# Two score passes of the next batch ahead of a w_in stage in a fused attention and GELU-MLP kernel

## The chip, the cores and the metric

The kernel runs on one core of one Trainium2 chip. The metric is the device time of one execution in microseconds (us). Beside it stands one profiled execution: its trace has the start and duration of every instruction on TensorE (PE; its weight loads are PEld), VectorE (DVE), ScalarE (ACT), GpSimd (POOL) and the DMA issues of SyncE (SP).

## What is computed

The inputs are q, k and v of 8 batches x 12 heads x 448 tokens x 64, and two weight matrices. Attention with normalised q and k is followed by two matrix products with an exact GELU between them.

```python
q_n = q / (np.linalg.norm(q, axis=-1, keepdims=True) + 1e-06)
k_n = k / (np.linalg.norm(k, axis=-1, keepdims=True) + 1e-06)
scores = np.matmul(q_n, k_n.transpose(0, 1, 3, 2)) / tau
attn = softmax(scores)                      # over the last axis
x = (attn @ v).transpose(0, 2, 1, 3).reshape(B * S, H * D)   # 3584 x 768
h = x @ w_in                                # 768 x 2048
g = 0.5 * h * (1 + erf(h / sqrt(2)))
out = g @ w_out                             # 2048 x 768, float32
```

## The kernel before

**Units of work.** Batches are counted from 0 to 7 and quads (four heads) from g = 0 to 23, three a batch. A quad's q and k are prepared in a chain: load (L129, SP), squares (L156, POOL), sums of squares (L165, DVE), logarithm and the exponential of half of it (L172 and L181, ACT), adding 1e-6 and the reciprocal (L190 POOL, L192 DVE), scaling to bf16 (L208, two POOL instructions) and a DMA transpose (L220, SP). Quad g is unit g+1 in the code, since quad 0 is cut in two. Units that share the small instructions L172 to L192 are a "group".

A quad's scores are 7 passes, 21 in a batch. A pass (L246) is 4 matmuls of 64x64 that run side by side into one pair of PSUM banks, and one exponential on ACT (L253), which frees the pair. There are 8 banks: pairs 0, 1 and 2 and two single banks ("mm"). After a quad's 7 exponentials `both` makes the row sums (L275, 16 matmuls of 128x32, into an mm bank), the values (L289, 28 matmuls of 64x64, into a pair) and on DVE the reciprocals and the two products with x (L297 to L323).

**Stages.** `attention(b)` alternates score passes of batch b with runs of matmuls of the second product (L352, "op", called fill), left over from batch b-1. A run takes as many as `plan` says: 96 in all for odd b, 128 for even b. Then `first(b)` is the w_in stage: 96 matmuls (L642, "hp") in 16 column blocks and 16 GELUs (L678). The first few blocks (`ahead`) do their first four steps of six before any does the last two, which need the batch's last quad. PE runs all of this in the order in which the code issues it. Exponential and GELU need different ACT tables, so that ACT loads a table ahead of the w_in stage (L634) and behind it (L687).

**Order around the change.** Every engine runs its instructions in program order and waits only on semaphores; tiles come from pools of a few buffers (q and k 4, scaled quads 3, transposed quads 3, exponentials 15). `upto(f, n)` issues step f up to item n at that point. Before, `group(b, k)` issues passes in eight parts of 3, 3, 3, 2, 3, 3, 2, 2; part 0 stands behind the w_in stage of b-1 and the others lie among the six runs of `attention(b)`. Batch 0 has an order of its own (L405), and during it POOL issues the casting loads of the weights wi (L381) and wo (L388) and of v (L141), while SP issues the loads of q and k.

Of the kernel before, what the change touches and what calls it, by code (L numbers as in the profile page):

```python
# [16 lines left out]
def kernel(  # L17
# [20 lines left out]
    NQ = H // 4  # L38
# [66 lines left out]
    def pair(i, name):  # L105
        pool = third[0] if i == 2 else ps_st
        return pool.tile([128, 2, 512], F32, tag=f"st{i}", name=name)
# [3 lines left out]

    units = [(0, 0, 1), (0, 1, 2)] + [(g, 0, 2) for g in range(1, NG)]
    NU = len(units)
    groups = [[n] for n in range(NQ + 2)] + [[NQ + 2, NQ + 3]]
    for n in range(2 * NQ + 1, NU, NQ):
        groups += [[n, n + 1], [n + 2]]
    shapes = [[len(gr), 2, units[gr[0]][2] - units[gr[0]][1], C] for gr in groups]
    place = {u: (n, j) for n, gr in enumerate(groups) for j, u in enumerate(gr)}
    qk_t, v_t, sq_t, nq_t, rn_t, qkb_t, qkT_t, pt_t = {}, {}, {}, {}, {}, {}, {}, {}
# [139 lines left out]
    def sums(g, chunks=range(C)):  # L259
        for c in chunks:  # L260
            if c == 0:
                bank_t[g, "sm"] = ps_acc.tile([128, 512], F32, tag="sm", name=f"sm{g}") if g < NQ else \
                    mm_tile(f"sm{g}", aside=0)
            for s in range(2):
                if g < NQ:
                    nc.tensor.matmul(bank_t[g, "sm"][64 * s:64 * (s + 1), :S],
                                     lhsT=ones2.rearrange("p a h r -> p (a h r)"), rhs=pt_t[g, s, c],
                                     start=(c == 0), stop=(c == C - 1), tile_position=(0, 64 * s))
                    continue

                half = 2
                for i in range(2) if c == half else ((c - (c > half)) % 2,):
                    r = 32 * (2 * s + i)
                    cols = slice(i * S // 2, (i + 1) * S // 2) if c == half else slice(0, S)
                    nc.tensor.matmul(bank_t[g, "sm"][r:r + 32, cols], lhsT=ones, rhs=pt_t[g, s, c][:, cols],  # L275
                                     start=(c < 2), stop=(c >= C - 2), tile_position=(0, r))
# [18 lines left out]
    def turned(g):  # L295
        tr = rcp.tile([128, NB, 32], F32, tag="tr", name=f"tr{g}")
        nc.vector.transpose(tr.rearrange("p b r -> p (b r)"), bank_t.pop((g, "sm"))[:, :S])  # L297
        bank_t[g, "tr"] = tr.rearrange("p b (k r) -> p k b r", k=2)

    def inverted(g):  # L300
        tr = bank_t.pop((g, "tr"))
        if g < NQ:
            su = tr[:, :, :, 0]
        else:


            for j in range(4):
                o = j ^ 1
                nc.vector.tensor_reduce(tr[32 * j:32 * (j + 1), :, :, 1], tr[32 * o:32 * (o + 1), :, :, 0:1],  # L309
                                        mybir.AxisListType.X, ALU.add)  # L310
            su = rcp.tile([128, 2, NB], F32, tag="su", name=f"su{g}")
            nc.vector.tensor_reduce(su, tr[:, :, :, 0:2], mybir.AxisListType.X, ALU.add)
        rc = bank_t[g, "rc"] = rcp.tile([128, 2, NB], F32, tag="rc", name=f"rc{g}")
        nc.vector.reciprocal(rc, su)

    def spread(g, h):
        rs = rcp.tile([128, NB, 32], F32, tag=f"rs{h}", name=f"rs{g}_{h}")
        nc.vector.transpose(rs, bank_t[g, "rc"][:, h].to_broadcast([128, NB, 32]))  # L318
        rs_t[g, h] = rs.rearrange("p b r -> p (b r)")
# [5 lines left out]
    def both(g, p):  # L325
        sums(g)
        turned(g)
        inverted(g)
        spread(g, 0)
        spread(g, 1)  # L330
        values(g, p=p)
        normalise(g, 0)
        normalise(g, 1)
# [60 lines left out]
    def upto(f, n, last=None):  # L394
        last = {load_qk: NG, load_v: NV, root: len(groups), load_wi: 4, load_wo: 4}.get(f, NU)
        while done.get(f, 0) < min(n, last):
            done[f] = done.get(f, 0) + 1
            f(done[f] - 1)
# [173 lines left out]
        done.update({square: 6, reduce: 5, root: 5, scale: 5, transposes: 5})  # L572


    passes = [(n, c) for n in range(NQ) for c in range(C)]
    group_pairs = [(0, 1, 2), (0, 1, 2), (0, 1, 2), (1, 2), (1, 2, 0), (1, 2, 0), (2, 0), (2, 0)]

    def group(b, k):
        n0 = sum(len(p) for p in group_pairs[:k])
        for p, (n, c) in zip(group_pairs[k], passes[n0:]):  # L580
            scores(b * NQ + n, ((0, c), (1, c)), p)
            exps(b * NQ + n, ((0, c), (1, c)))

    def attention(b, fill):
        fill = list(fill)
        plan = {96: (20, 13, 13, 12, 16, 22), 128: (24, 18, 20, 18, 22, 26)}[len(fill)]
        parts = iter(plan)

        def run():
            for _ in range(next(parts)):  # L590
                fill.pop(0)()

        x_t[b] = xp.tile([128, KD, S], BF16, tag="x", name=f"x{b}")
        g0, nu = b * NQ, (b + 1) * NQ + 1
        run()
        for n in (nu - 1, nu):
            upto(scale, n)
            upto(transposes, n)
        group(b, 1)
        upto(square, nu + 1)  # L600
        run()
        group(b, 2)
        both(g0, 0)
        upto(load_v, b + 3)
        if b == 1:
            upto(load_qk, g0 + NQ + 2)
        group(b, 3)
        upto(square, nu + 2)
        run()
        group(b, 4)  # L610
        upto(reduce, nu + 1)
        upto(load_qk, g0 + NQ + 3)
        run()
        group(b, 5)
        both(g0 + 1, 1)
        group(b, 6)
        run()
        group(b, 7)
        upto(reduce, nu + 2)
        n = 2 * b + 4  # L620
        if n < len(groups):
            logs(n)
            roots(n)
        run()
        both(g0 + 2, 1)
        if n < len(groups):
            inverses(n)
            done[root] = n + 1

    def first(b):  # L630
        sb, hf = divmod(b, 2)
        if hf == 0:
            g_t[sb] = gp.tile([128, KF, 2 * S], BF16, tag="g", name=f"g{sb}")
        nc.scalar.preload_act_table_set(GELU_SET)  # L634
        nu = (b + 1) * NQ + 1
        hps = {}
        pairs = (0, 2) if b else (0, 2, 6, 8)
        ahead = 4 if b else 5

        def mm(m, kds):  # L640
            for kd in kds:
                nc.tensor.matmul(hps[m], lhsT=wi[:, kd, m * 128:(m + 1) * 128],  # L642
                                 rhs=x_t[b][:, kd, :], start=(kd == 0), stop=(kd == KD - 1))

        def bank(m):
            if m in pairs:
                p = (2, 0)[m // 2] if b else (1, 0, 1, 0)[pairs.index(m)]
                st = pair(p, f"hp{b}_{m}")
                hps[m], hps[m + 1] = st[:, 0, :S], st[:, 1, :S]
            elif m not in hps:  # L650
                hps[m] = mm_tile(f"hp{b}_{m}")[:, :S]

        for m in range(ahead):
            bank(m)
            mm(m, range(KD - 2))
        if b == 0:
            upto(square, nu + 3)
        for n in (nu + 1, nu + 2) if b else (nu + 1,):
            upto(scale, n)
            upto(transposes, n)  # L660
        if b:
            upto(load_qk, (b + 1) * NQ + 5)
        else:
            upto(load_wo, 4)
        upto(square, nu + 3)
        upto(reduce, nu + 3)
        for m in range(ahead):
            mm(m, range(KD - 2, KD))
        for m in range(KF):
            if b == 0 and m == 8:  # L670
                for i in range(2):
                    transposes(4, i)
                    copies(4, i)
            if m >= ahead and (m == 0 or m - 1 not in pairs):
                for k in range(m, m + 1 + (m in pairs)):
                    bank(k)
                    mm(k, range(KD))
            nc.scalar.activation(g_t[sb][:, m, hf * S:(hf + 1) * S], hps.pop(m), AF.Gelu)  # L678
            if b == 0 and m == 5:
                nc.scalar.preload_act_table_set(EXP_SET)  # L680
                upto(root, 6)
                nc.scalar.preload_act_table_set(GELU_SET)
                upto(scale, nu + 2)
                upto(transposes, nu + 2)
                upto(load_qk, 2 * NQ + 1)
        if b + 1 < B:
            nc.scalar.preload_act_table_set(EXP_SET)  # L687
            group(b + 1, 0)
            upto(root, 2 * b + 6)

    upto(load_qk, 1)
    nc.scalar.preload_act_table_set(EXP_SET)
# [7 lines left out]
    fill = []  # L700
    for b in range(B):
# [12 lines left out]
        fill = [f for t, ni in todo if t not in tail for f in second_pieces(sb, t, ni)]  # L714
# [38 lines left out]
```

## Time and profile before

| what | value |
|---|---|
| time, median of 4 runs | 418.26 us (417.54 to 418.69) |
| the profiled execution: its time | 418.69 us |
| its span, first to last instruction | 416.9 us |
| granted TensorE clock | 0.998 |
| busy: PE, ACT, DVE, POOL | 98%, 59%, 45%, 40% |
| start of the w_in stage of batch 0 to 3 | 32.71, 80.68, 132.05, 178.44 us |
| start of the w_in stage of batch 4 to 7 | 229.81, 276.20, 327.57, 373.96 us |

From one w_in start to the next it takes 51.37 us where the fill is 128 and 46.39 us where it is 96, each time alike from the second on; the first such stretch, from batch 0 to batch 1, is 47.97 us.

A line of the timeline gives start, duration, engine, line and operation, output<-inputs, shapes and count; in brackets is the idle time ahead of it and what ended it. Ends of matmuls are modelled, so that stretches on PE are taken from one start to the next. In the list of DMA queues, q0 holds what POOL issues and q1 what SP issues.

### The profile page before, as it was taken

How to read it: one execution, taken by the hardware profiler on the slowest of the kernel's cores; microseconds unless marked ns; L12 is line 12 of the kernel's file. 1: busy time of each engine (PE TensorE's matmuls, PEld its weight loads, DVE VectorE, ACT ScalarE, POOL GpSimd, SP SyncE). 2: the span in 40 equal slices, each digit the busy share in tenths (PEclk: the TensorE clock that was granted, in tenths of full speed). 3: DMA queues.
4: the chain of work that ended last, by engine and by line, in shares of the span. 5: the costliest groups of instructions: out<-in, count | busy, mean ns of one | idle time of the engine just before them, and what ended most of it. 6: DMA issues, size and time to landing. Idle time of an engine off the chain costs nothing.

```text
span 416.9 us, 8254 instructions
## 1 busy us (share of the span) xinstructions
PE 409.3 (98%) x3506; PEld 212.2 (51%) x3506; DVE 188.3 (45%) x379; ACT 246.4 (59%) x358; POOL 167.3 (40%) x113
## 2 busy tenths in 40 slices
PE   7999999999999999999999999999999999999996
PEld 3445545555555554554555555455555554555564
DVE  5687128801676026741276314861167511661021
ACT  6995687356663578735864359735866348844300
POOL 4999606090900909053540636317280272000000
PEclk9999999999999999999999999999999999999999
DMA  8999999445473546729192382936375150430033
GB/s 279 263 258 207 203 213 268 115 79 188 89 186 77 92 173 99 180 58 244 28 224 64 75 230 42 196 77 141 126 138 176 38 90 0 85 75 2 0 77 76
DMA packets 66516, 54.53 MB, mean 131 GB/s; under 512 B 38576, under 2 KB 61488, under 8 KB 66480
## 3 DMA queue, kind: packets, MB, share of 16 engines
q1 hardware_dynamic: 53984, 41.79, 39.4%
q0 software_dynamic: 12112, 11.80, 17.8%
q8 instruction: 27, 0.44, 0.4%
q10 hardware_dynamic: 384, 0.43, 0.4%
q14 instruction: 9, 0.07, 0.1%
HBM read 45.61 MB, written 11.01 MB: 136 GB/s over the span
## 4 chain that ended last, share of the span: by engine, by line
PE 85%; POOL 7%; DMA 3%; issue 3%; DVE 1%; ACT 0%; POOLq 0%
PE op L352 33%; PE hp L642 31%; PE st L246 8%; PE o L289 7%; PE sm L275 4%; POOL qkb L208 4%; DMA qkT<-qkb 3%; PE op L367 1%; POOL sq L156 1%; POOL wi L381 1%; POOL v L141 1%; DVE nq L165 0%; POOL wo L388 0%; POOL se L190 0%; DVE rn L192 0%
## 5 line engine op out<-in xcount | busy, mean ns | idle before, releaser
L253 ACT ACTIVATE pt<-st 128x896 bf16<-128x896 f32 x168 | 142.9, 916 | 40.4 <-PE st L246 39.5
L352 PE MATMUL op<-wo,g 128*128 128x384 bf16 x864 | 147.9, 327 | 0.0
L642 PE MATMUL hp<-x,wi 128*128 128x448 bf16 x768 | 146.8, 353 | 0.0
L678 ACT ACTIVATE g<-hp 128x448 bf16<-128x448 f32 x128 | 66.7, 545 | 99.4 <-PE hp L642 99.1
L352 PEld LDWEIGHTS <-g 128*128 128x128 bf16 x864 | 81.1, 98 | 63.2 <-issue 12.7
L642 PEld LDWEIGHTS <-wi 128*128 128x128 bf16 x768 | 74.4, 98 | 71.4 <-issue 2.9
L208 POOL TENSOR_TENSOR qkb<-qk,rn 128x896 bf16<-128x896 f32 (+1 forms) x49 | 79.6, 1652 | 46.1 <-DVE rn L192 46.1
L165 DVE TENSOR_REDUCE nq<-sq 128x28 f32<-128x1792 f32 (+2 forms) x30 | 48.8, 1637 | 64.1 <-POOL sq L156 61.3
L156 POOL TENSOR_TENSOR sq<-qk 128x1792 f32<-128x1792 f32 (+1 forms) x22 | 66.8, 3042 | 14.1 <-DMA qk<-in_k_dram 14.0
L356 DVE COPY ot<-op 128x384 f32<-128x384 f32 x54 | 29.5, 546 | 69.6 <-PE op L352 69.6
L190 POOL TENSOR_SCALAR se<-sr 128x28 f32<-128x28 f32 (+1 forms) x14 | 4.4, 313 | 122.2 <-ACT sr L181 122.2
L246 PE MATMUL st<-qkT 64*64 64x448 bf16 x672 | 48.5, 359 | 1.4 <-DMA qkT<-qkb 0.8
L289 PE MATMUL o<-pt,v 64*64 64x448 bf16 x672 | 36.9, 352 | 0.0
L246 PEld LDWEIGHTS <-qkT 64*64 64x64 bf16 x672 | 18.2, 105 | 27.0 <-issue 18.1
L192 DVE RECIPROCAL rn<-se 128x28 f32<-128x28 f32 (+2 forms) x18 | 6.8, 376 | 51.3 <-POOL se L190 51.1
L297 DVE STREAM_TRANSPOSE tr<-sm 128x448 f32<-128x448 f32 x24 | 15.6, 650 | 29.2 <-PE sm L275 26.1
L318 DVE STREAM_TRANSPOSE rs<-rc 128x448 f32<-128x448 f32 x48 | 28.1, 623 | 0.8
L323 DVE TENSOR_TENSOR x<-o,rs 128x448 bf16<-128x448 f32 x48 | 27.0, 599 | 1.0 <-DVE rs L318 0.5
L289 PEld LDWEIGHTS <-v 64*64 64x64 bf16 x672 | 17.7, 106 | 15.9 <-issue 7.3
L275 PE MATMUL sm<-pt,ones 128*32 128x448 bf16 (+1 forms) x336 | 19.1, 332 | 0.0
L309 DVE TENSOR_REDUCE tr<-tr 32x28 f32<-32x28 f32 x84 | 16.5, 196 | 1.6
L275 PEld LDWEIGHTS <-ones 128*32 128x32 bf16 x336 | 7.3, 95 | 10.3 <-issue 8.5
(43 smaller groups left out, 118.5 us busy)
## 6 DMA issues: line engine op xcount, KB each, us to landing
out_dram<-ot SPq DMA_DIRECT2D x54, 192.0 KB, 2.9
qk<-in_q_dram SPq DMA_DIRECT2D x23, 448.0 KB, 6.0
qk<-in_k_dram SPq DMA_DIRECT2D x23, 448.0 KB, 6.6
v<-in_v_dram POOLq DMA_DIRECT2D x7, 672.0 KB, 10.9
wi<-in_moe_w_in_dram POOLq DMA_DIRECT2D x8, 384.0 KB, 14.9
wo<-in_moe_w_out_dram POOLq DMA_DIRECT2D x4, 768.0 KB, 15.0
qk<-in_q_dram SPq DMA_DIRECT2D x2, 224.0 KB, 3.4
v<-in_v_dram POOLq DMA_DIRECT2D x1, 448.0 KB, 9.6
```

Of the source, the lines that this page charges most:

```text
L156: eng.tensor_tensor(sq[:, part], t[:, part], t[:, part], ALU.mult)
L165: nc.vector.tensor_reduce(nq[:, part], sq[:, part], mybir.AxisListType.X, ALU.add)
L208: eng.tensor_tensor(qkb[:, i, :, s0:s1].rearrange("p c s d -> p s c d"), t[:, i, s0:s1], rn[:, i].to_broadcast([128, s1 - s0, C, D]), ALU. ...
L246: nc.tensor.matmul(st[cols, n, :S], lhsT=qkT[rows, 1, c, cols], rhs=qkT[rows, 0, :, cols], start=True, stop=True, tile_position=(64 * s, 6 ...
L253: nc.scalar.activation(pt[:, :m], st[:, :m, :S], AF.Exp, scale=inv_tau)
L275: nc.tensor.matmul(bank_t[g, "sm"][r:r + 32, cols], lhsT=ones, rhs=pt_t[g, s, c][:, cols], start=(c < 2), stop=(c >= C - 2), tile_position ...
L289: nc.tensor.matmul(bank_t[g, h][cols, :S], lhsT=v_t[g][rows, s, c, :], rhs=pt_t[g, s, c][rows], start=(c == 0), stop=(c == C - 1), tile_po ...
L318: nc.vector.transpose(rs, bank_t[g, "rc"][:, h].to_broadcast([128, NB, 32]))
L352: nc.tensor.matmul(ps[:, :NH], lhsT=g_t[sb][:, kf, t * 128:(t + 1) * 128], rhs=wo[:, kf, ni * NH:(ni + 1) * NH], start=(kf == 0), stop=(kf ...
L356: nc.vector.tensor_copy(ot[:, ni * NH:(ni + 1) * NH], ps[:, :NH])
L642: nc.tensor.matmul(hps[m], lhsT=wi[:, kd, m * 128:(m + 1) * 128], rhs=x_t[b][:, kd, :], start=(kd == 0), stop=(kd == KD - 1))
L678: nc.scalar.activation(g_t[sb][:, m, hf * S:(hf + 1) * S], hps.pop(m), AF.Gelu)
```

## The change

The passes of a batch are dealt out anew: two stand at the end of `attention(b-1)`, behind the last values and in front of the w_in stage; then 3, 3, 3, 5 and 5 follow in `attention(b)`, where 5 is 3 ahead of a `both` and 2 behind it. Batch 1 alone still has its first three behind the w_in stage of batch 0, and two instead of three in its third part. The runs are cut anew. The w_in stage takes other banks, and `ahead` is 6 instead of 4. The last quad of a batch shares a group with the first quad of the next, and the second quad has a group to itself; the preparing steps move accordingly. The load of g = 6 (quad 0 of batch 2) moves from behind the transpose of g = 4 in the w_in stage of batch 0 to its start.

```diff
-    groups = [[n] for n in range(NQ + 2)] + [[NQ + 2, NQ + 3]]
-    for n in range(2 * NQ + 1, NU, NQ):
-        groups += [[n, n + 1], [n + 2]]
+    groups = [[n] for n in range(NQ + 2)] + [[NQ + 2, NQ + 3], [2 * NQ + 1]]
+    for n in range(2 * NQ + 2, NU, NQ):
+        groups += [[n], [n + 1, n + 2] if n + 2 < NU else [n + 1]]
...
-    group_pairs = [(0, 1, 2), (0, 1, 2), (0, 1, 2), (1, 2), (1, 2, 0), (1, 2, 0), (2, 0), (2, 0)]
...
+    at = {}
+    def visit(b, pairs):
+        for p in pairs:
+            n, c = passes[at.get(b, 0)]
+            at[b] = at.get(b, 0) + 1
             scores(b * NQ + n, ((0, c), (1, c)), p)
             exps(b * NQ + n, ((0, c), (1, c)))
     def attention(b, fill):
-        plan = {96: (20, 13, 13, 12, 16, 22), 128: (24, 18, 20, 18, 22, 26)}[len(fill)]
+        plan = {96: (16, 14, 16, 18, 16, 16), 128: (20, 18, 20, 22, 32, 16)}[len(fill)]
...
-        g0, nu = b * NQ, (b + 1) * NQ + 1
+        g0, u = b * NQ, b * NQ + 1
         run()
-        for n in (nu - 1, nu):
-            upto(scale, n)
-            upto(transposes, n)
-        group(b, 1)
-        upto(square, nu + 1)
+        upto(scale, u + 3)
+        upto(transposes, u + 3)
+        upto(square, u + 4)
+        upto(load_qk, g0 + NQ + 2)
+        upto(reduce, u + 4)
+        visit(b, (0, 1, 2))
+        upto(root, 2 * b + 5)
+        upto(scale, u + 4)
+        upto(transposes, u + 4)
         run()
-        group(b, 2)
+        visit(b, (0, 1, 2))
+        run()
+        upto(load_qk, g0 + NQ + 3)
+        visit(b, (0, 1) if b == 1 else (0, 1, 2))
+        upto(square, u + 5)
+        run()
+        visit(b, (0, 1, 2))
         both(g0, 0)
         upto(load_v, b + 3)
-        if b == 1:
-            upto(load_qk, g0 + NQ + 2)
-        group(b, 3)
-        upto(square, nu + 2)
+        upto(load_qk, g0 + NQ + 4)
+        visit(b, (1, 2))
+        upto(reduce, u + 5)
         run()
-        group(b, 4)
-        upto(reduce, nu + 1)
-        upto(load_qk, g0 + NQ + 3)
-        run()
-        group(b, 5)
+        visit(b, (1, 2, 0))
         both(g0 + 1, 1)
-        group(b, 6)
-        run()
-        group(b, 7)
-        upto(reduce, nu + 2)
-        n = 2 * b + 4
+        visit(b, (2, 0))
+        n = 2 * b + 5
         if n < len(groups):
             logs(n)
             roots(n)
         run()
-        both(g0 + 2, 1)
+        both(g0 + 2, 2)
         if n < len(groups):
             inverses(n)
             done[root] = n + 1
+            visit(b + 1, (0, 1))
     def first(b):
...
-        nu = (b + 1) * NQ + 1
+        u = (b + 1) * NQ + 1
-        pairs = (0, 2) if b else (0, 2, 6, 8)
-        ahead = 4 if b else 5
+        pairs = {2: 0, 4: 1} if b else {0: 1, 2: 0, 6: 1, 8: 0}
+        ahead = 6 if b else 5
...
         if b == 0:
-            upto(square, nu + 3)
-        for n in (nu + 1, nu + 2) if b else (nu + 1,):
-            upto(scale, n)
-            upto(transposes, n)
-        if b:
+            upto(load_qk, 2 * NQ + 1)
+            upto(square, u + 3)
+            upto(scale, u + 1)
+            upto(transposes, u + 1)
+            upto(load_wo, 4)
+            upto(reduce, u + 3)
+        else:
+            upto(scale, u + 2)
+            upto(transposes, u + 2)
             upto(load_qk, (b + 1) * NQ + 5)
-        else:
-            upto(load_wo, 4)
-        upto(square, nu + 3)
-        upto(reduce, nu + 3)
+            upto(square, u + 4)
+            upto(reduce, u + 4)
...
-                upto(scale, nu + 2)
-                upto(transposes, nu + 2)
-                upto(load_qk, 2 * NQ + 1)
+                upto(scale, u + 2)
+                upto(transposes, u + 2)
         if b + 1 < B:
             nc.scalar.preload_act_table_set(EXP_SET)
-            group(b + 1, 0)
-            upto(root, 2 * b + 6)
+            if b == 0:
+                visit(1, (0, 1, 2))
+            else:
+                upto(root, 2 * b + 7)
```

More of the change, by code (lines that the diff above doesn't have):

```diff
@@ L575 @@
     passes = [(n, c) for n in range(NQ) for c in range(C)]
-    group_pairs = [(0, 1, 2), (0, 1, 2), (0, 1, 2), (1, 2), (1, 2, 0), (1, 2, 0), (2, 0), (2, 0)]
-    def group(b, k):
-        n0 = sum(len(p) for p in group_pairs[:k])
-        for p, (n, c) in zip(group_pairs[k], passes[n0:]):
+    at = {}
[3 more added lines that the diff above has]
+            at[b] = at.get(b, 0) + 1
             scores(b * NQ + n, ((0, c), (1, c)), p)
@@ L646, in bank @@
             if m in pairs:
-                p = (2, 0)[m // 2] if b else (1, 0, 1, 0)[pairs.index(m)]
-                st = pair(p, f"hp{b}_{m}")
+                st = pair(pairs[m], f"hp{b}_{m}")
                 hps[m], hps[m + 1] = st[:, 0, :S], st[:, 1, :S]
```

## The prediction

> **What bounds the kernel now.** First the busy rows and the chain that ended last: PE is busy for 98% of the span and holds 85% of the chain; before 60 us the chain is POOL and one DMA transpose.
>
> ```profile
> PE 409.3 (98%) x3506; PEld 212.2 (51%) x3506; DVE 188.3 (45%) x379; ACT 246.4 (59%) x358; POOL 167.3 (40%) x113
> PE 85%; POOL 7%; DMA 3%; issue 3%; DVE 1%; ACT 0%; POOLq 0%
> ```
>
> A busy PE can still lose time between kinds of matmul, so next the timeline of PE. This is the w_in stage of batch 4 and half of attention(5), a stretch of fill 96:
>
> ```profile
> 229.81 18.34 PE L642 MATMUL hp<-x,wi 128*128 128x448 bf16 x96
> 248.07 0.76 PE L246 MATMUL st<-qkT 64*64 64x448 bf16 x12
> 248.76 3.42 PE L352 MATMUL op<-wo,g 128*128 128x384 bf16 x20
> 252.12 0.88 PE L246 MATMUL st<-qkT 64*64 64x448 bf16 x12
> 252.93 2.29 PE L352 MATMUL op<-wo,g 128*128 128x384 bf16 x13
> 255.15 0.79 PE L246 MATMUL st<-qkT 64*64 64x448 bf16 x12
> 255.87 1.05 PE L275 MATMUL sm<-pt,ones 128*32 128x448 bf16 x16
> 256.85 1.52 PE L289 MATMUL o<-pt,v 64*64 64x448 bf16 x28
> 258.20 0.55 PE L246 MATMUL st<-qkT 64*64 64x448 bf16 x8
> 258.68 2.29 PE L352 MATMUL op<-wo,g 128*128 128x384 bf16 x13
> ```
>
> Start to start, 20 op matmuls take 3.36 and 13 take 2.22: 0.163 each and 0.10 left over when the kind changes. An hp matmul is 18.26 / 96 = 0.19, and so is a pass (four side by side): 12 score matmuls should take 0.57 and take 0.69, so 0.12 to 0.13 go at leaving them. A detached score block thus costs 0.10 + 0.13 = **0.23**. Values into scores is cheap: 28 values are 1.33 and take 1.35.
>
> Two rows here hold a wait as well: the scores at 252.12 take 0.81 instead of 0.69, and the sums at 255.87 take 0.98, where the later ones of the stretch take 0.78 (273.97 to 274.75). ACT says why: it loads its table behind the last GELU and begins the first exponentials at 250.03, 2 us behind their scores, so the pairs come free late.
>
> ```profile
> 248.74 1.28 ACT L687 ACT_TABLE_LOAD   x1
> 250.03 2.54 ACT L253 ACTIVATE pt<-st 128x896 bf16<-128x896 f32 x3
> ```
>
> Last, the one idle stretch of PE behind 45 us, in attention(1), and SP's queue, where it comes from: the transpose of g = 4 issues at 46.81 and lands at 60.00.
>
> ```profile
> 58.83 0.38 PE L246 MATMUL st<-qkT 64*64 64x448 bf16 x4
> 60.04 0.57 PE L246 MATMUL st<-qkT 64*64 64x448 bf16 x8 [0.83 <-DMA qkT<-qkb]
> ```
>
> ```profile
> 46.81 4.67 SPq L220 DMA_TRANSPOSE qkT<-qkb  x1
> 51.59 0.51 SPq L129 DMA_DIRECT2D qk<-in_q_dram  x1
> 52.78 8.86 SPq L220 DMA_TRANSPOSE qkT<-qkb  x1
> ```
>
> **The change, stages of batches 2 to 7.** PE's matmuls stay the same in number. Behind the w_in stage the block of three scores is gone: hp goes straight into op, both 128x128, and 0.23 falls away. Its passes join blocks: two stand behind the values ahead of hp. Values into scores costs 0.02; scores into hp is not in the trace, bounded by 0.02 (values into scores) and 0.13 (scores into op, values into hp, 229.81 - 228.35 - 1.33). I take 0.13, since the tile size changes, and it replaces the 0.13 of values into hp. Net -0.21 a stage.
>
> The waits for late exponentials go too, because ACT has its table back 1.95 us behind w_in's end and the first scores now come 16 or 20 op later (2.7 or 3.35 us); the passes that were late are exponentiated ahead of the GELUs. In stretches of 96 that is 0.12 + 0.03 + 0.20 + 0.11 (a second block of 0.80, 260.89 to 261.69) = 0.46, less rounding and 0.04 for one more wait like the 0.52 of the scores at 266.56; in those of 128 the sums alone wait (205.82 to 206.82, 0.23), less 0.04. Sum: **-0.62** in three stretches of 96 (batches 3, 5, 7) and **-0.40** in three of 128 (2, 4, 6): -3.06.
>
> What hides the rest. Scores ahead of hp hold pairs 0 and 1: the first exponential follows its scores by 0.44 and takes 0.92, so pair 0 is free 1.36 after; hp's third block, which wants it, starts 0.53 + 8 x 0.19 = 2.05 after. Pair 1: 2.2 against 3.6. Without that cover each us late is a us of PE, six times. The last DVE products (3.05 us into the stage, 229.81 to 232.85) were met by 4 x 4 hp matmuls (3.04); now 6 x 4 (4.6). The table load for GELU ends about 3.0 us in, ahead of the first GELU at 4.9. Quad 0 of the next batch must be transposed some 10 us earlier: root at 250.0 + 0.6, POOL and DVE 0.9, two scalings 6.63, landing 4.0: 262, needed at 276. Quad 2's scaling leads it and lands at 259 against 263.7. In the w_in stage POOL has one scaling and two squares (9.7) for two and one (9.8). SP's new transpose goes into a buffer that quad 0's last passes read; they are over (E + 6.5, where E is w_in's end) before POOL has scaled (E + 10.4), so the stores and loads queued behind it on SP wait for POOL, not for that, and the third output tile is stored 1 to 6 us later, with 3 buffers of 32 matmuls each to spare.
>
> **Batch 1** pays. The load of g = 6 (two of 448 KB, 512 pieces of 1792 bytes) leaves SP when POOL has scaled g = 2 (21.8 us), 30 us earlier, behind g = 5, whose last piece lands at 32.87; it then runs among wi and wo.
>
> ```profile
> q0 software_dynamic: 292, 0.55, 72.1%
> q1 hardware_dynamic: 293, 0.50, 37.7%
> ...
> q0 software_dynamic: 224, 0.42, 111.8%
> ...
> q0 software_dynamic: 755, 0.57, 91.1%
> q1 hardware_dynamic: 745, 0.19, 35.9%
> ```
>
> The three are 24 to 28, 32 to 34 and 51 to 55 us. The queues take turns piece by piece: q0 does 73 a us beside q1 and 112 alone, so 512 / 73 = 7 us of company put POOL's loads back by 7 x 0.35 = 2.5 us. The last of wi lands at 37.84, then 40.4; its block starts at 42.6: hidden. The first half of wo lands at 46.0, then 48.6, wanted at 52: hidden. But wo's second half now keeps company with the transpose of g = 4 to its end. Its pieces begin at 50.7 (none of q1 from 46.5 to 50.7); 1792 pieces (half of the 3648 that two transposes in 87 to 95 us show with other small ones) at 745 / 4 = 186 a us take 9.65: 60.35 instead of 60.00, where the company thinned out from 56. At best it lands before PE needs it; at worst, if q0 took two pieces to one, 16 us of transfer and 67.
>
> PE wants g = 4 at: w_in's end 51.75 + 0.70 + 16 op 2.71 = 55.16; there the third pass waits for the third exponential (53.72 + 2.54 = 56.26); scores done 56.6; 14 op 2.38; one pass: 59.2. It starts at **60.45** for 60.04, with 30 op done instead of 33. From there to the w_in stage it was 80.68 - 60.04 = 20.64; now 3 op more (0.49), one wait less (0.12), 0.05 of small change, and 0.40 for the two passes of batch 2, which come back in the last stage. So batch 1 loses 0.41 + 0.42 = +0.83. One wait is new here: ACT's logarithm for g = 6 stands between two blocks of exponentials. Its square can run at 50.1, when POOL has scaled, to 53.3; DVE sums it behind the first op copy (55.3 to 55.9, then 2.0), done at 57.9; ACT is free for it at 58.8. If the sum came later, the exponentials behind it would wait, and PE's scores for them.
>
> **Sum:** -3.06 + 0.83 = **-2.2 us**. On the profiled execution's own 418.69 that is 416.5; this execution lies 0.43 above the median, 418.26, so I predict **416.1**.
>
> Two rules of the Trainium skill speak against it. The granted clock is 1.00 in 58.83 to 60.04, idle and all; the idle stretch now grows from 0.83 to some 1.3 us. "TensorE: Matmul & The Clock Gate", section "What's actually happening", halves the clock after about 3.4 us idle; by that, nothing here, and by an estimate from its figure 1.7 us more if the wait grew so long. And "DMA: Bandwidth & Descriptors", section "Issuing engines are not separate DMA queues", says that transfers of all engines share the same 16 and interleave: by it an earlier load is never free, as the rows above show; it gives no sum of its own.
>
> **Rivals.** (1) *Better:* the transpose of g = 4 lands before 59.2, because wo is not behind after all: 1.25 more, 414.8. For: the 1792-byte pieces themselves slowed its tail. Against: the piece counts are equal. 0.10. (2) *Slower:* the same transpose is pushed back by wo's delayed loads. From a landing of 62.6 on nothing is gained, from 63.5 it is slower by over 0.2%; at 67 the time is 422.7. For: that chain ended last already. Against: one to one, 1792 pieces cannot last longer than 9.65. 0.07. (3) *A new wait takes the place:* hp's banks behind the exponentials, or the preparation of the joint group; 0.3 to 0.4 a stage would eat the gain: 418. Against: the slacks above (0.7, 1.4, 4.6 us). 0.06. (4) *It doesn't do what it says:* leaving scores for hp costs more, or the waits only move to the blocks of five, and half is left: 417.2. 0.09. The forecast keeps 0.68.
>
> About 0.2% (0.8 us) is what a measurement can tell from no change. Faster: forecast, (1) and (4), 0.87; same 0.06; slower 0.07. The range takes in (1) and (4): 414.6 to 417.6.
>
> **What would show it.** Right: w_in stages 50.9 and 45.7 apart from batch 1 on; op directly behind hp; sums at 0.78; a PE idle stretch of over 1 us before g = 4's first pass, at 60.3 to 60.6; w_in of batch 1 at about 81.9. Wrong: idle time on PE in front of hp, hp above 18.3, GELU behind 5 us, g = 4 landing elsewhere, or the last of wi behind 42.6.

## The result

| | before | changed |
|---|---|---|
| median | 418.08 us (60 executions) | 419.51 us (38) |
| ratio of the two | | 1.0029, 95% interval 1.0020 to 1.0038 |
| profiled execution: time, span | 418.69, 416.9 us | 417.7, 415.8 us |
| its mean granted clock | 0.998 | 1.000 |

The change makes the kernel 0.3% slower; 416.1 was predicted, 0.5% faster. The profiled execution is nevertheless 1.0 us faster than before's. Both hold, because these 38 and the profiled one fall into two kinds: 30 have a mean granted clock of 0.992 to 0.996 and a median of 419.7; 9 have 0.999 to 1.000 and a median of 418.0. The profile shown first below is one of the 9. So two things want an answer: where the predicted 2.2 us went in an execution at full clock, and what takes 1.7 us more in the others. Of the runs further down, two hold one execution each of some 838 us and one holds six of 426.5 to 427.1 us; the ratios leave these eight out.

### The profile page after: what moved, and what is told of

The parts are those of the page before. It is cut to its first block, busy times and chain, and to the rows that moved or that the text cites. A ratio compares the mean times of both kernels' runs of the same rounds, so it can differ in the third digit from the quotient of the medians.

```text
span 415.8 us, 8256 instructions
## 1 busy us (share of the span) xinstructions
PE 406.4 (98%) x3506; PEld 212.5 (51%) x3506; DVE 188.8 (45%) x380; ACT 246.8 (59%) x360; POOL 167.2 (40%) x114
## 4 chain that ended last, share of the span: by engine, by line
PE 84%; POOL 8%; DMA 4%; issue 1%; DVE 1%; ACT 0%; POOLq 0%
PE op L352 33%; PE hp L647 31%; PE st L246 8%; PE o L289 7%; PE sm L275 4%; POOL qkb L208 4%; DMA qkT<-qkb 4%; POOL sq L156 2%; PE op L367 1%; POOL wi L381 1%; DMA qk<-in_q_dram 1%; DVE nq L165 1%; POOL wo L388 0%; POOL v L141 0%; ACT lq L172 0%
## 5 line engine op out<-in xcount | busy, mean ns | idle before, releaser
L275 PE MATMUL sm<-pt,ones 128*32 128x448 bf16 (+1 forms) x336 | 17.8, 332 | 0.0
L403 PE MATMUL spin<-blank,ident 128*128 128x448 bf16 x34 | 9.7, 429 | 2.0 <-DVE root L89 1.9
```

## Profile after

The busy rows and the chain hardly differ: PE does the same work, with less busy time at the borders between kinds.

```profile
PE 406.4 (98%) x3506; PEld 212.5 (51%) x3506; DVE 188.8 (45%) x380; ACT 246.8 (59%) x360; POOL 167.2 (40%) x114
PE 84%; POOL 8%; DMA 4%; issue 1%; DVE 1%; ACT 0%; POOLq 0%
```

**The regular stages** are as forecast. PE's timeline of the w_in stage of batch 6 and half of attention(7), fill 96:

```profile
327.45 18.33 PE L647 MATMUL hp<-x,wi 128*128 128x448 bf16 x96
345.62 2.76 PE L352 MATMUL op<-wo,g 128*128 128x384 bf16 x16
348.32 0.76 PE L246 MATMUL st<-qkT 64*64 64x448 bf16 x12
349.01 2.45 PE L352 MATMUL op<-wo,g 128*128 128x384 bf16 x14
...
358.51 0.76 PE L246 MATMUL st<-qkT 64*64 64x448 bf16 x12
359.20 0.85 PE L275 MATMUL sm<-pt,ones 128*32 128x448 bf16 x16
359.98 1.52 PE L289 MATMUL o<-pt,v 64*64 64x448 bf16 x28
361.33 0.59 PE L246 MATMUL st<-qkT 64*64 64x448 bf16 x8
361.85 2.77 PE L352 MATMUL op<-wo,g 128*128 128x384 bf16 x16
```

op starts directly behind hp. Every block of 12 scores takes 0.69 and the sums 0.78 from start to start; the waits of 0.12 and 0.20 in the corresponding lines of before are gone.

**Batch 1** is not. PE's timeline in attention(1), then SP's:

```profile
58.79 0.38 PE L246 MATMUL st<-qkT 64*64 64x448 bf16 x4
61.69 0.57 PE L246 MATMUL st<-qkT 64*64 64x448 bf16 x8 [2.52 <-DMA qkT<-qkb]
```

```profile
21.63 0.37 SPq L129 DMA_DIRECT2D qk<-in_q_dram  x1
22.04 0.47 SPq L129 DMA_DIRECT2D qk<-in_k_dram  x1
46.60 13.69 SPq L220 DMA_TRANSPOSE qkT<-qkb  x2
```

The load of g = 6 leaves SP at 21.63 and nothing stands between the two transposes. The first, of g = 4, issues at 46.60 (before: 46.81) but lands at 61.65 instead of 60.00, and PE's idle stretch grows from 0.83 to 2.52 us. The accounts close on that: the w_in stage of batch 1 starts at 83.12 instead of 80.68 (+2.44), and from there to the w_in stage of batch 7 it takes 289.70 instead of 293.28 (-3.58); the rest of the span is alike. Together -1.1 us of span and, with 0.14 more outside it, -1.0 of time.

**The clock.** A second profile of the same kernel (first run below) is one of the slower kind: 419.80 us, clock 0.996. Its stretches while PE waits, behind the wait, and after (behind the stretch come its length and PE's busy time; the third number from the end is the granted clock):

```profile
59.58:62.16 2.58, 0.39 (x7) 0.12 (x6) 0.33 (x1) 1.05 (x2) 1.84 (x2) 1.00 1.32 127
62.53:65.94 3.41, 3.41 (x18) 1.54 (x12) 0.56 (x1) 1.73 (x2) 1.40 (x1) 0.50 1.58 336
66.00:70.00 4.00, 4.00 (x31) 2.10 (x30) 0.56 (x1) 1.73 (x2) 1.98 (x1) 1.00 0.75 210
```

For 3.41 us, 0.4 us after PE has work again, the clock is at one half. On PE's timeline the 16 op matmuls that fall in it take 4.27 us from start to start; elsewhere they take 2.70:

```profile
62.16 0.64 PE L246 MATMUL st<-qkT 64*64 64x448 bf16 x8 [2.19 <-DMA qkT<-qkb]
62.73 4.34 PE L352 MATMUL op<-wo,g 128*128 128x384 bf16 x16
```

That is 1.6 of the 1.7 us between the two kinds.

Why the same wait halves the clock in one execution and not in another can be read from the clock's own records in the traces. Up to the first fall they have one stretch at full clock: 54.61 us here, 71.68 us in the run with more op ahead and 61.44 us in the one with wo's last quarter later, which is 16, 21 and 18 times 3.413. So in these traces the clock changes only at points 3.41 us apart. Cut at these points, the wait of the first profile (first two rows) is shared by two stretches, and that of the second (third row) lies in one:

```profile
57.38:60.79 3.41, 1.79 (x14) 0.80 (x11) 0.48 (x2) 2.43 (x5) 1.27 (x2) 1.00 1.32 181
60.79:64.20 3.41, 2.51 (x21) 1.38 (x22) 0.56 (x1) 1.73 (x2) 2.34 (x2) 1.00 1.16 280
59.12:62.53 3.41, 1.22 (x16) 0.35 (x13) 0.33 (x1) 1.48 (x4) 2.21 (x3) 1.00 1.32 155
```

PE is idle for 1.62 and 0.90 us of the first two, and the clock stays; it is idle for 2.19 us of the third, and the next stretch is at one half. In the profiles here, every such stretch with up to 1.62 us of waiting was followed by the full clock, and those with 2.14, 2.19 and 3.35 us by half of it; what lies between was not measured.

## Experiments

**Theory 1:** the early load puts wo's loads back, these keep the transpose of g = 4 company (they run among its pieces) to its end, PE idles for 2.5 us, and this idling halves the clock for 3.4 us in most executions. **Theory 2:** the lower clock has another cause, somewhere in the new order. "Low clock" below counts executions under 0.9975; medians and ratios are against executions of before on the same chip (418.0 to 418.2).

### The changed kernel again

> The changed kernel once more, to see its spread and, if its profiled execution is one of the slow-clocked ones, where the clock falls. Theory 1 (idle PE): the 2.5 us in which PE waits for the transpose of g = 4 lowers the granted clock in most executions; a profile with a mean clock of 0.995 then shows matmuls at twice their duration in the few us behind 61.7 us and nowhere else, and some 1.5 to 2 us lost there. Theory 2 (rival): the clock falls for another cause, a place in the regular stages (scores ahead of hp); the long matmuls then stand there. Median 419.5 for both.

Measured: 419.66 us, ratio 1.0036 (1.0019 to 1.0053), low clock in 10 of 12. The half clock stands where theory 1 has it (shown above), and nowhere else.

### Dummy matmuls in the wait

```diff
+        if b == 1:
+            visit(b, (0,))
+            spin(12)                  # and spin(5) in the second run
+            visit(b, (1, 2))
+        else:
             visit(b, (0, 1, 2))
```

> The changed kernel with 12 dummy matmuls (448 columns, 2.3 us) between the two first passes of the third score block of batch 1, where PE idles for 2.5 us anyway. No other work moves. Theory 1: the clock stays at 1.00 in nearly all executions, and the median comes to that of the full-clock executions of the changed kernel, 417.6 to 418.3. Theory 2: clocks of 0.995 as before, median 419.5.

> The changed kernel with 5 dummy matmuls (0.95 us) in the wait instead of 12, so that some 1.4 us of idle PE are left. Theory 1 with a limit between 1 us (before, no fall) and 2.5 us: the share of executions with a clock of 0.995 says on which side 1.4 lies; if it is none, the median is 418.0 as with 12; if most, 419.5. Theory 2 is out if the clock follows the idle time.

Measured: with 12, 418.03 us, ratio 0.9996 (0.9977 to 1.0015), low clock in 0 of 12; with 5, 417.87 us, ratio 1.0000 (0.9988 to 1.0011), low clock in 1 of 12. PE's timeline with 12 and with 5:

```profile
60.48 2.44 PE L403 MATMUL spin<-blank,ident 128*128 128x448 bf16 x12
63.56 0.57 PE L246 MATMUL st<-qkT 64*64 64x448 bf16 x8 [0.64 <-DMA qkT<-qkb]
```

```profile
59.19 1.12 PE L403 MATMUL spin<-blank,ident 128*128 128x448 bf16 x5
61.65 0.57 PE L246 MATMUL st<-qkT 64*64 64x448 bf16 x8 [1.35 <-DMA qkT<-qkb]
```

g = 4 comes no earlier and PE goes on no earlier; only the idling is shorter. With 0.64 and 1.35 us of it the clock stays up in 23 of 24 executions, with 2.2 to 2.5 it is halved in most. Theory 2 is out. The 418.0 that is left is before's time: without the fall of the clock, the change still gains nothing at the median.

### More op ahead of the wait

```diff
+        if b == 1:
+            plan = (20, 30, 12, 12, 11, 11)
```

> The changed kernel with the runs of attention(1) cut as 20, 30, 12, 12, 11, 11 instead of 16, 14, 16, 18, 16, 16: 20 more op matmuls (3.3 us) ahead of g = 4's first pass, so that the wait is filled with work that has to be done anyway. Theory 1: no wait over 0.5 us, clock 1.00, and the 2.5 us wait and the 0.7 us wait for exponentials come back: 415.0 to 415.8. Theory 2: the wait's 2.5 us come back too, but the lower clock stays: 417.

Measured: 418.13 us, ratio 1.0004 (0.9985 to 1.0023), low clock in 6 of 12 (median of those 419.1, of the others 417.3); 415.0 to 415.8 had been expected. The wait for g = 4 is down to 0.46 us, but a new one stands 13 us later. PE's timeline, DVE's, and the clock of the two stretches:

```profile
75.03 0.38 PE L246 MATMUL st<-qkT 64*64 64x448 bf16 x4 [0.22 <-DVE x L323]
77.42 1.50 PE L275 MATMUL sm<-pt,ones 128*32 128x448 bf16 x16 [2.00 <-DVE ot L356]
```

```profile
74.91 2.00 DVE L165 TENSOR_REDUCE nq<-sq 128x28 f32<-128x1792 f32 x1
76.83 0.55 DVE L356 COPY ot<-op 128x384 f32<-128x384 f32 x1
```

```profile
74.80:77.42 2.62, 0.40 (x8) 0.20 (x4) 2.57 (x3) 2.42 (x3) 0.00 (x0) 0.98 1.01 333
77.42:80.80 3.38, 3.38 (x40) 1.49 (x43) 1.69 (x7) 0.00 (x0) 0.00 (x0) 0.51 1.22 220
```

With the shorter runs, the sum of squares of g = 7 on DVE stands ahead of a copy that frees the bank for the row sums. PE idles 2.0 us and the half clock follows again, at another place and for another reason: idling is the cause, not the transpose.

### The early load alone, in the kernel before

```diff
         if b == 0:
+            upto(load_qk, 2 * NQ + 1)
             upto(square, nu + 3)
```

> The kernel before with one part of the change alone: the load of g = 6 at the start of the w_in stage of batch 0 instead of behind the transpose of g = 4. If the early load alone puts the transpose back (through wo's delayed loads), it lands at 61.6 instead of 60.0, PE idles some 2.5 us, the span grows by 1.65, and by theory 1 the clock falls in most executions: 419.7 at full clock, median some 421.3. If the order on SP's queue (the next transpose directly behind) is what makes it late, it does that too here, since the load no longer stands between; if neither, it lands at 60.0 and the time is that of before, 418.1. Theory 2: full clock, 419.7 at most.

Measured: 421.34 us, ratio 1.0092 (1.0058 to 1.0126), low clock in 5 of 6. g = 4's first pass on PE:

```profile
60.86 0.57 PE L246 MATMUL st<-qkT 64*64 64x448 bf16 x8 [2.06 <-DMA qkT<-qkb]
```

One line of the change, in the old order of passes, is enough for the wait and, in most executions, for the low clock; the profiled one is the one of six at full clock. From the start of the w_in stage of batch 0 to that pass it takes 28.57 us, where before has 27.33 and the changed kernel 29.19 and 28.87 in two profiles.

### wo's second half, or its last quarter, loaded later

```diff
             upto(scale, u + 1)
             upto(transposes, u + 1)
-            upto(load_wo, 4)
+            # half: no line here; quarter: upto(load_wo, 3)
...
         upto(reduce, u + 4)
+        upto(load_wo, 4)
         visit(b, (0, 1, 2))
```

> The changed kernel with the load of wo's second half issued behind the square of g = 6 in attention(1) (about 53 us) instead of at 39.4 us in the w_in stage. If wo's delayed pieces are what keeps the transpose of g = 4 company, it now has the DMA engines nearly to itself and lands at 53 to 55; PE has no wait ahead of g = 4's first pass, which starts at 59.0 for 61.7, the clock stays at 1.00 in nearly all executions, and the median comes to 415.0 to 415.6. wo's second half has to land by 63; if it doesn't, PE waits there instead. If the transpose is late for another reason (its issue, SP's order), it stays at 61 to 62 and the median at 419.5.

> The changed kernel with only the last quarter of wo issued later (behind the square of g = 6, about 53 us); the third stays at 39.4. The transpose of g = 4 then has company until some 56.4 and finishes alone: 1071 of its 1792 pieces by then, the rest at some 830 a us: 57.3, ahead of PE's 59.0. The last quarter is wanted at 64.3 and should land by 62 to 64, where all of the second half issued late landed at 67.2. No wait on PE over 0.5 us, full clock, median 415.0 to 415.6. If the last quarter is late again, a wait of up to 2 us stands there, and the median is 416 to 417.

Measured: half, 417.00 us, ratio 0.9982 (0.9966 to 0.9997), low clock in 0 of 11; quarter, 421.90 us, ratio 1.0078 (1.0048 to 1.0109), low clock in 5 of 6. Both miss the 415.0 to 415.6 that were expected, the half although its wait for g = 4 is gone. The transpose lands at 53.39 with half of wo out of its way and at 57.16 with a quarter (57.3 was expected), with the two transposes issued back to back in both, so SP's order is not what delays it: wo's pieces are. But the bill comes at wo. PE's timelines, half and quarter:

```profile
67.19 1.46 PE L352 MATMUL op<-wo,g 128*128 128x384 bf16 x8 [1.82 <-DMA wo<-in_moe_w_out_dram]
```

```profile
69.96 2.72 PE L352 MATMUL op<-wo,g 128*128 128x384 bf16 x8 [5.39 <-DMA wo<-in_moe_w_out_dram]
```

The last quarter takes from 53.03 to 69.92; the load of g = 7 and the next transposes run beside it now, which is the likely reason. The 5.4 us of idling cost the clock as well.

Four more runs are of this kind. With the half later and a plan of 20, 16, 12, 16, 16, 16:

> The changed kernel with wo's second half later as above, and runs of 20, 16, 12, 16, 16, 16 in attention(1), so that the third pass of its second block finds its pair free. If the wait for late exponentials (0.5 to 0.7 us) is real time there, 0.4 to 0.6 us below the run with wo alone; if PE only waits elsewhere instead, the same.

Measured 418.25 us, ratio 1.0003 (0.9987 to 1.0019), low clock in 4 of 12: not below the run with wo alone but 1.25 us above it, and the wait for wo grows to 2.42 us. With the quarter later and that plan:

> The same with runs of 20, 16, 12, 16, 16, 16 in attention(1): the 0.7 us that PE waits for the exponentials' pairs in the second block is filled with op matmuls. If the run above has no other wait, 0.3 to 0.6 us less than it; if wo's last quarter is what ends last, no difference.

Measured 421.82 us over five executions, ratio 1.0093 (1.0079 to 1.0108), low clock in 5 of 5; the profiled execution is the sixth, of 838 us, so there is only the time. As expected for a wo that ends last, it does not differ from the run without the plan. And the same edits in the kernel before (`upto(load_wo, 4)` behind its scaling in attention(1)):

> The kernel before with the load of wo's second half issued behind the scaling of g = 5 (about 50 us). g = 4's first pass starts at 58.9 to 59.1 instead of 60.04 in the profiled execution of before: the wait goes, and the median falls by what of it is usual in before, 0.3 to 1.0 us, to 417.1 to 417.7. Together with the run above, the difference between the two is what the rest of the change is worth without the wait: 2.2 to 2.7 us.

> The kernel before with the last quarter of wo issued later (about 50 us). Its wait ahead of g = 4's first pass, 0.8 us in the profiled execution, goes: 417.2 to 417.8. What lies between this and the changed kernel with the same edit is what the order of passes is worth by itself: 2.2 to 2.7 us.

Measured: half, 424.15 us over all 12, low clock in 9 of them. Six lie at 426.5 to 427.1 with a clock of 0.991 or 0.992, and no trace shows one of these; the other six have a median of 420.7 and the ratio 1.0058 (1.0035 to 1.0082). The profiled one, at full clock, waits 2.06 us for wo. Quarter: 418.18 us over 11, ratio 1.0015 (0.9990 to 1.0039), low clock in 2 of 11, no difference, though its profiled execution has no wait and 417.59 us. Both expectations failed: late wo can hurt more than the wait that it removes. These runs therefore give no clean price for the order of passes; the next one comes closer.

### The order from batch 2 on

```diff
-    groups = [[n] for n in range(NQ + 2)] + [[NQ + 2, NQ + 3], [2 * NQ + 1]]
-    for n in range(2 * NQ + 2, NU, NQ):
+    groups = [[n] for n in range(NQ + 2)] + [[NQ + 2, NQ + 3], [2 * NQ + 1, 2 * NQ + 2], [3 * NQ], [3 * NQ + 1]]
+    for n in range(3 * NQ + 2, NU, NQ):
...
-        visit(b, (0, 1) if b == 1 else (0, 1, 2))
+        visit(b, (0, 1) if b == 2 else (0, 1, 2))
...
-            attention(b, fill)
-        first(b)
+            (attention if b > 1 else attention_old)(b, fill)
+        (first if b > 1 else first_old)(b)
```

`attention_old` and `first_old` are the functions of before; the load of g = 9 and the square and sum of unit 10 stand one stage earlier in them.

> The changed kernel's order from batch 2 on; the w_in stage of batch 0, attention(1) and the w_in stage of batch 1 stay as before, with the load of g = 6 where it was, so that nothing is added among wi and wo. (g = 9 is loaded, squared and summed one stage earlier, as quad 0 of batch 3 needs a group of its own here.) If the early load and the wait behind it are all that went wrong, g = 4's first pass starts where it does in before, the clock stays at 1.00, the stages of batches 3 to 7 take 45.75 and 50.95 as in the changed kernel, that of batch 2 some 51.5, and the median is 415.2 to 415.8. If the order itself costs something that the single profile did not show, the median stays above 416.5.

Measured: **415.17 us**, ratio 0.9938 (0.9920 to 0.9957), low clock in 0 of 6. This version beats both. Four executions lie at 414.8 to 415.3 and two at 417.2 and 417.7; the last is the profiled one. Of its 2.5 us above the median, some 1.5 may lie ahead of the w_in stage of batch 0, which starts at 34.21 there (32.71 in before's profile). g = 4's first pass starts 27.52 us behind that, as in before (27.33), behind an idle stretch of 1.01 us. PE's timeline at two w_in stages:

```profile
134.18 18.33 PE L647 MATMUL hp<-x,wi 128*128 128x448 bf16 x96
152.34 2.76 PE L352 MATMUL op<-wo,g 128*128 128x384 bf16 x16
...
179.92 2.25 PE L647 MATMUL hp<-x,wi 128*128 128x448 bf16 x11
```

45.74 apart, as in the changed kernel; the next two stages take 50.95 and 45.74. The stage of batch 2, which takes the part that batch 1 has in the change, takes 51.80. From g = 4's first pass to the end of the span it takes 354.13 us; in before 356.84, in the changed kernel 354.06.

## Why the prediction was wrong

**Right:** the bound and the price of a border (0.23 a detached block). Stages of 50.94 and 45.75 us were measured for 50.9 and 45.7. Scores into hp cost 276.51 - 276.03 - 0.38 = 0.10 (0.13 was assumed). No wait came in front of hp, and from the w_in stage of batch 1 on PE waited for no other engine and no transfer. wi's last load landed at 39.65 (40.4 was estimated) and stayed hidden. From the w_in stage of batch 1 to that of batch 7 the change gives 3.58 us; 3.06 and the 0.40 of the two passes that come back, 3.46, were predicted.

**The term that was mis-sized** is the landing of g = 4's transpose. The mechanism was named (piece by piece, wo in company to the end), but 1792 pieces were shared out evenly: 9.65 us (1792 / 186 is 9.63), so 60.35. It landed at 61.65. The lists of DMA queues of the changed kernel, 50 to 60, 59 to 60 and 60 to 61.6 us, show that this was no bound:

```profile
q1 hardware_dynamic: 1950, 0.49, 36.1%
...
q0 software_dynamic: 149, 0.11, 68.8%
q1 hardware_dynamic: 389, 0.10, 59.8%
...
q1 hardware_dynamic: 650, 0.16, 114.9%
q0 software_dynamic: 60, 0.04, 16.4%
```

By 60 us SP's queue has moved 1950 pieces, more than this transpose has, and in the last of these us twice the 188 a us that it had in company; yet the transpose is not done, so pieces of the next one must have gone ahead of some of its own. The trace has 16 completions for each transfer: those of wo's last load come from 60.68 to 61.67 and the transpose's from 60.86 to 61.65, and PE goes on behind the last. This fits 16 engines that are not equally far. No view shows them one by one, and the first completion, too, comes 0.5 us behind 60.35, so the rest of the 1.3 us stays open.

Further, the sum was made against a single profiled execution of before. In it, it takes 356.84 us from g = 4's first pass to the end; taken from the median of before's spans (416.2 us on one chip) that puts the pass at an estimated 59.4, not 60.04. Part of this may be a shorter wait and part an earlier start: in the profiles here the w_in stage of batch 0 starts anywhere from 32.3 to 34.2 us. The same estimate for the 12 dummy matmuls (median span 416.05, 354.04 from that pass) gives 62.0. By these estimates the early load costs some 2.6 us there at the median, nearly all that the later stages give: 2.8 (356.84 - 354.04). The run from batch 2 on, which lacks the early load, agrees: it is 2.8 us below the full-clock executions of the changed kernel (415.17 and 418.0).

**The step that failed** is the one on the clock: "by that, nothing here". The row behind it showed a clock of 1.00 through a wait of 0.83 us and cannot speak for a longer one. The page of the Trainium skill cited there, "TensorE: Matmul & The Clock Gate", section "What's actually happening", puts the fall at about 3.4 us of idle PE; here 2.0 to 2.5 us sufficed in most executions. The length of the half-clock stretch, 3.41 us, is that page's window. The measurement decides: on this kernel a wait of up to 1.35 us cost its own length, and one of 2.0 to 2.5 us cost up to 1.7 us more, where some 2.1 us of idling fell into one stretch of 3.41. Of the 3.4 us between 416.1 and 419.5, some 1.5 are the clock (419.5 against 418.0 at full clock) and 1.9 the landing, with the one execution that it was reckoned from.

**The rivals.** The second, the same transpose pushed back by wo, is what came. What was held against it, that 1792 pieces cannot last longer than 9.65 us, did not hold: from 50.7 to 61.65 they took 10.95. It was priced by its landing alone: its point of no gain was put at 62.6 us, and by the profile alone 61.65 still gains 1.0. With the clock it decides earlier. Rival 4 (half is left) looks like the profiled execution, for another reason. Rivals 1 and 3 did not come, save that in the run with more op a new wait did take the place of the old.

## What to carry to other kernels

A transfer that is moved forward into a stretch where the DMA engines are full is paid for by whatever is last there: ask which wait that one ends, allow for a landing later than an even share of the pieces gives, and look at more than one execution. A wait on PE is not worth its length only; one that grows past what the profile has shown at full clock may halve the clock behind it, so give its price with and without that. Where a regular order gains and its first round loses, start it one round later.

## What the runs showed that was not expected

The clock splits executions of one kernel into two kinds 1.7 us apart, and the one profile may be of the rarer kind: the count of clocks over all executions was the first clue. DMA engines can be busy and move little: in the run with wo's last quarter later, from 58 to 61 us the core moved 73 GB/s, against 191 in the company of 51 to 55 us.

```profile
DMA packets 602, 0.22 MB, mean 73 GB/s; under 512 B 477, under 2 KB 602, under 8 KB 602
q1 hardware_dynamic: 477, 0.12, 111.5%
q0 software_dynamic: 125, 0.10, 33.1%
```

A piece of q1 takes 1.115 x 16 x 3 / 477 = 0.11 us there; the pieces of 87 to 95 us in before, mostly transposes, take 0.722 x 16 x 8 / 3692 = 0.025. Both times transposes run; here SP has issued a plain load behind them at 56.77. Before is nearly as slow at 57.5 to 59.5 us (92 GB/s), where plain loads of SP stand between two transposes. That the two kinds of transfer disturb each other was not tried by itself and stays open.
